# Attention with a soft mixture of experts on one core: small VectorE steps on one input stream, half of the low parts on GpSimd, mask and second fold split by head

## The chip, the cores and the metric

The kernel runs on one core of a Trainium2 chip. The core has five engines that work side by side, each through its own list of instructions in order: TensorE (PE in the profile, its weight loads PEld), VectorE (DVE), ScalarE (ACT), GpSimd (POOL) and SyncE (SP), which here issues all DMA transfers. They meet through semaphores. The metric is the time of one execution on the device, in microseconds (us).

## The reference

Eight sequences, eight heads, 576 positions, head dimension 64; then a soft mixture of eight experts with four slots each.

```python
scores = scale * np.matmul(q, k.transpose(0, 1, 3, 2))
cum = np.cumsum(np.maximum(s, 0.0), axis=-1)
bias = -(cum[:, :, :, None] - cum[:, :, None, :])
scores = np.where(causal, -1000000000.0, scores + np.minimum(bias, 0.0))
scores = scores - np.max(scores, axis=-1, keepdims=True)
attn = np.exp(scores)
attn = attn / (np.sum(attn, axis=-1, keepdims=True) + 1e-09)
attn_out = np.matmul(attn, v)
...
logits = x @ phi                       # x: (4608, 512), the heads side by side
d = softmax of logits over the rows    # dispatch; 32 columns
slot_input = d.T @ x
h = np.maximum(slot_input[e] @ w1[e], 0.0);  slot_out[e] = h @ w2[e]
c = softmax of logits over the columns # combine
out = c @ slot_out
```

## The kernel before, in words

Two heads (a = 0, 1) are one pair; there are 32 pairs p, four to a sequence, so eight batches b of four pairs. The attention loop runs over the pairs in a software pipeline and is followed by an expert part at the end. The names below are the keys of the operations (`op((name, p, ...), engine, ...)`) in the code.

For each pair: `load` brings q and k, transposed. `cast` (ACT) rounds them to the fast matmul format into a tile `w`, and `low` (line 453, DVE) subtracts, for queries (0) and keys (1), the rounded part from the original, so that products keep their accuracy: 64 calls on 128x576. `mx` (line 479, PE) makes approximate scores, four groups; `red` (line 493, DVE) adds the bias row `ub` from a DMA or, on the diagonal blocks, the masked copy `mk` of it, and takes the running maximum of each row. `mk` (line 432, POOL) makes that copy for both heads with two selects. `fm` (line 509, DVE) joins the two kinds of maximum into 20 columns `mh`; `f1` (line 514, PE) transposes them into `mt`; `f2` (ACT) and `f3` (line 524, DVE) split them in two parts `hl`; `md` writes these by DMA as extra rows beside the queries. Then `s` (line 550, PE) makes the scores with the maximum subtracted, `ex` (line 561, ACT) the exponentials, `cut` (line 568, POOL) zeroes what lies above the diagonal, `a` and `ax` (lines 643, 632, PE) multiply by the values.

The sums of the rows come from `za` (line 589), which adds two column blocks of the exponentials, head 0 on DVE and head 1 on POOL, from `z` (line 594, POOL), which folds in the third block from column group ZT = 4 on, both heads in one instruction of 2x320, and from `sm` (line 690, PE), which adds up the rest with a column of ones: 26 calls for a pair, which the profile counts as 52 matmuls. Every four pairs `e1` inverts the sums, a DMA pair `rw`, `rd` spreads them, `nr` (line 720, DVE) multiplies, and `nat`, `lt`, `c0` to `t8` update the expert logits and slots: `t2` (line 909) keeps the running minimum `nmin`, `t4` (line 927) the running sums `tot`, both on DVE with one or two columns.

What stands where in an engine's list is not written as a loop. A table gives each operation a place (a number for each kind, pair in the batch and type of batch), each engine's operations are sorted by it, and the function `timeline` merges the five lists with assumed durations, waits and a shared port of DVE and POOL. So the order inside each engine is fixed by the table alone. Short `busy` matmuls fill the start.

Of the kernel before, what the change touches and what calls it, by code (L numbers as in the profile page):

```python
# [13 lines left out]
ALU = mybir.AluOpType  # L14
# [11 lines left out]
ZT = 4  # L26
ZA = ("DVE", "POOL")

PERIOD = 38813
# [4 lines left out]
def table(text):  # L34
# [24 lines left out]
    low.0.0=-145512,-24218,-8235,-6404,-2495 cast.0.1=-128151,-13019,-9675,-10190,-5528
    low.0.1=-157331,-25864,-2554,-8208,-993 cum.0=-172132,3336,-5029,-2032,-7884  # L60
    mx.0.0=-131561,-13342,-2588,-8179,-2006 red.0.0.0=-130092,-17572,-1404,-3987,-2097
    red.0.0.1=-111753,-17989,-692,-3140,-2388 mx.0.1=-109409,-25895,-8267,-2275,-6484
    red.0.1.0=-120494,-22879,-3533,-2310,-5047 red.0.1.1=-132160,-23102,-3734,-2556,-7413
    mx.0.2=-182983,-12289,-790,795,1721 red.0.2.0=-115681,-15771,295,-165,1799 red.0.2.1=-113861,-5723,556,142,887
    mx.0.3=-90966,-2683,-739,1203,1628 red.0.3.0=-109993,-12133,974,107,756 red.0.3.1=-109885,-5704,1376,-210,1594
    fm.0=-109528,-2668,1624,1624,2297 f1.0=-86204,2876,7567,7523,10430 f2.0=-57637,-692,5807,5457,6581
    f3.0=-103916,3609,4834,2606,2954 md.0=-34002,9267,586,-1466,14239 s.0.0=-38951,14281,18571,20321,19184
    ex.0.0.0=-29427,16804,19505,18458,25033 ex.0.0.1=-26773,18031,19178,19412,23352
    cut.0.0=-105027,14062,17131,17024,21912 s.0.1=-44622,9375,15456,14386,18741
    ex.0.1.0=-39699,7602,18222,16186,22367 ex.0.1.1=-30923,10391,18102,17550,21966  # L70
    cut.0.1=-84485,8456,25066,19381,26094 s.0.2=-33057,17079,24080,22649,23834 ex.0.2.0=-9848,22550,24591,24608,28689
    ex.0.2.1=-9963,23174,24483,25538,28796 cut.0.2=-38055,14513,23950,20367,28508
    s.0.3=-38462,14628,23746,22649,21888 ex.0.3.0=-21484,18404,23936,21693,25606
    ex.0.3.1=-13247,21282,23727,23784,27494 cut.0.3=-38856,14194,18296,24860,31558
    za.0.0=-26432,23637,23749,21924,23432 za.0.1=-34684,18632,27777,25649,31493 z.0=-31754,20580,28351,30229,33192
    load_v.0=-166175,11282,12370,-153,12086 ax.0=-11237,23556,28279,25181,29500 evx.0=11009,23180,27183,29947,36125
    a.0.0=-30003,24119,25021,23376,25440 a.0.1=-15869,24133,26086,24741,28916 a.0.2=-15122,25617,27262,24978,30055
    a.0.3=-11096,26323,28058,25025,30813 a.0.4=-10535,26386,28379,25207,30960 ev.0=11844,28093,28120,30073,36400
    sm.0=678,27230,29412,29297,31087 rd.0=59666,61270,62920,64506,72341 nr.0=69670,70046,70115,69026,71358
    nat.0=69017,75129,73492,84383,78259 natd.0=69001,73241,77003,84760,98898  # L80
    load.1=-176331,-20047,-14277,-13193,-13109 ub.1=-79298,-9932,-9560,-9037,-8449
    mk.1=-112557,-14420,-2370,-6296,7120 cast.1.0=-125098,-4710,926,2478,3681 low.1.0=-135642,1399,7732,5391,2379
    cast.1.1=-90784,-2076,2080,3831,3729 low.1.1=-87008,5993,5799,5880,7841 cum.1=-75193,9964,6847,1104,17061
    mx.1.0=-65390,3350,10844,10876,12104 red.1.0.0=-66999,5531,7279,4194,7744 red.1.0.1=-59177,4739,7602,5128,6486
    mx.1.1=-48226,4979,11728,11495,13566 red.1.1.0=-81203,6332,7808,6343,9753 red.1.1.1=-72360,6946,8106,6446,10104
    mx.1.2=-44807,10990,15837,15272,14227 red.1.2.0=-58350,8322,12156,9208,11490
    red.1.2.1=-57220,8930,12813,12298,12329 mx.1.3=-73555,5275,15307,14146,15570
    red.1.3.0=-65406,7836,8773,6969,13629 red.1.3.1=-71098,9100,10270,8038,13444 fm.1=-56381,9503,13793,14035,15003
    f1.1=-40585,13083,18441,19461,19252 f2.1=-37646,16557,18858,18318,20199 f3.1=-48895,10151,14925,15709,15675
    md.1=-26222,12372,13204,11670,22553 s.1.0=-25920,23739,25038,23480,26146 ex.1.0.0=-1511,23454,24650,28195,32856  # L90
    ex.1.0.1=-766,25287,25010,28750,32245 cut.1.0=-33334,20326,28607,29130,41622 s.1.1=-26778,24442,25237,23677,26113
# [138 lines left out]
def tile_attn_softmoe(ctx: ExitStack, tc, qk, v, s, phi, w1, w2, cst, out):  # L230
# [10 lines left out]
    NCH = 5  # L241
# [133 lines left out]
    def own(kind, i, n):  # L375
        live[kind, i % n] = i
# [926 lines left out]
```

## Time and profile before

| | us |
|---|---|
| three runs: median, lowest, highest | 445.18, 443.41, 445.39 |
| the profiled execution, its own time | 443.02 |
| its span from first to last instruction | 441.2 |
| busy in it: PE / DVE / ACT / POOL | 398.7 / 355.4 / 240.3 / 218.2 |

The span is 1.8 us shorter than the execution's own time. The attention loop fills roughly the stretch from 35 to 346 us; from 381 us on the expert part runs. TensorE's granted clock was 0.978 over the whole span and 1.00 in the loop, its upper level, 2.4 GHz.

### The profile page before, as it was taken

Reading aid. Unit: us, or ns where it says so; the run is one execution under the profiler, and the core shown is the slowest. Engines: PE = TensorE matmul, PEld = TensorE weight load, DVE = VectorE, ACT = ScalarE, POOL = GpSimd, SP = SyncE. Lnnn points to the kernel's source line nnn. Section 1 sums busy time; section 2 is a strip of 40 time slices with the busy share of each in tenths; the row PEclk is TensorE's granted clock in tenths of the full one; section 3 lists DMA queues with packets and bytes.
Section 4 is the critical chain, followed back from the end, with each engine's and each line's share of the span. In section 5 each row is a group of like instructions: output and inputs, shape, how many; then the busy total and the mean of one; then the engine's idle time right before and its main releaser. Section 6 shows DMA issues by size and latency. Waiting matters only on the chain.

```text
span 441.2 us, 17319 instructions
## 1 busy us (share of the span) xinstructions
PE 398.7 (90%) x6667; PEld 282.7 (64%) x6667; DVE 355.4 (81%) x1515; ACT 240.3 (54%) x703; POOL 218.2 (49%) x320
## 2 busy tenths in 40 slices
PE   8899989988899989988999889899989997899950
PEld 7776666775577657856776567666756855435740
DVE  6899899889999999899999999889999285211460
ACT  4165656564676576855685549465764646011350
POOL 5558667446576665656664566476656610000000
PEclk9899999999999999999999999999999999899995
DMA  5645556666676667666775675474748979999898
GB/s 165 237 177 172 160 185 190 188 223 206 165 229 219 223 166 239 241 220 219 222 218 172 203 250 192 151 237 148 239 155 239 329 267 363 343 404 409 307 340 296
DMA packets 40290, 102.64 MB, mean 233 GB/s; under 512 B 5456, under 2 KB 15568, under 8 KB 40208
## 3 DMA queue, kind: packets, MB, share of 16 engines
q1 hardware_dynamic: 40208, 101.53, 68.7%
q8 instruction: 53, 0.87, 0.8%
q14 instruction: 29, 0.24, 0.2%
HBM read 90.98 MB, written 10.17 MB: 229 GB/s over the span
## 4 chain that ended last, share of the span: by engine, by line
PE 54%; DVE 25%; issue 8%; DMA 4%; ACT 3%; POOL 2%; DVEq 0%; SPq 0%; POOLq 0%; ACTq 0%
PE s L550 17%; DVE junk L493 11%; PE y L643 9%; PE mx L479 5%; PE sum L690 4%; PE m L1137 4%; DVE w L453 3%; PE m L1169 3%; DVE mh L509 3%; PE nat L728 3%; PE busy L1096 2%; DMA arena<-in_v_dram 2%; DMA arena<-rs 2%; DVE arena L589 1%; DVE arena L720 1%
## 5 line engine op out<-in xcount | busy, mean ns | idle before, releaser
L493 DVE CUSTOM_DVE_ANT_0 junk<-mx,arena 128x320 uint8<-128x320 f32 (+4 forms) x576 | 160.2, 335 | 16.8 <-PE mx L479 13.6
L561 ACT ACTIVATE arena<-s 128x288 f32<-128x288 f32 (+4 forms) x384 | 121.4, 394 | 53.1 <-PE s L550 48.8
L568 POOL TENSOR_SCALAR_AFFINE_SELECT arena<-arena 128x256 f32<-128x256 f32 (+1 forms) x160 | 68.4, 446 | 96.8 <-ACT arena L561 96.3
L550 PE MATMUL s<-w 64*128 64x288 f32 (+4 forms) x1152 | 111.9, 304 | 2.1 <-DVE e_nat L841 1.3
L643 PE MATMUL y<-arena 128*32 128x320 f32 (+4 forms) x1280 | 108.8, 427 | 0.6 <-POOL arena L568 0.5
L550 PEld LDWEIGHTS s<-w 64*128 64x128 f32 (+1 forms) x1152 | 84.1, 176 | 19.4 <-issue 8.3
L594 POOL TENSOR_TENSOR arena<-arena 128x640 f32<-128x640 f32 x31 | 51.8, 1671 | 22.8 <-DVE arena L589 19.8
L550 PE MATMUL s<-g 64*128 64x288 f32 (+4 forms) x384 | 60.1, 290 | 0.0
L453 DVE TENSOR_TENSOR w<-arena,w 128x576 fp32r<-128x576 f32 x64 | 57.8, 909 | 0.1
L432 POOL TENSOR_SCALAR_AFFINE_SELECT arena<-arena 128x640 f32<-128x640 f32 x64 | 49.9, 803 | 15.2 <-DMA arena<-cumu 11.5
L479 PE MATMUL mx<-w 64*128 64x448 f32 (+4 forms) x384 | 51.7, 317 | 0.7 <-ACT arena L561 0.3
L643 PEld LDWEIGHTS y<-arena 128*32 128x32 f32 x1280 | 37.1, 109 | 21.7 <-issue 14.0
L493 DVE DVE_READ_ACCUMULATOR2_ANT mx<- 128x1 f32 x576 | 45.9, 80 | 0.0
L448 ACT CAST w<-arena 128x576 fp32r<-128x576 f32 x64 | 41.6, 683 | 4.3 <-DMA arena<-in_qk_dram 3.8
L479 PEld LDWEIGHTS mx<-w 64*128 64x128 f32 x384 | 34.7, 184 | 14.3 <-ACT arena L561 3.0
L589 POOL TENSOR_TENSOR arena<-arena 128x448 f32<-128x448 f32 x31 | 38.1, 1230 | 3.2 <-PE sum L690 3.0
L550 PEld LDWEIGHTS s<-g 64*128 64x128 f32 (+1 forms) x384 | 38.4, 177 | 0.3
L690 PEld LDWEIGHTS sum<-arena,onesl 128*32 128x32 f32 x1664 | 28.3, 110 | 7.4 <-issue 5.0
L589 DVE TENSOR_TENSOR arena<-arena 128x448 f32<-128x448 f32 x33 | 30.8, 933 | 0.6 <-POOL arena L568 0.3
L690 PE MATMUL sum<-arena,onesl 128*32 128x64 f32 x1664 | 31.2, 220 | 0.0
L520 ACT CAST hi<-mt 20x128 fp32r<-20x128 f32 x32 | 8.1, 255 | 40.4 <-PE mt L514 40.1
L720 DVE TENSOR_TENSOR arena<-arena 128x576 f32<-128x576 f32 x31 | 27.3, 885 | 3.4 <-DMA arena<-rs 3.3
(160 smaller groups left out, 490.5 us busy)
## 6 DMA issues: line engine op xcount, KB each, us to landing
arena<-in_qk_dram SPq DMA_DIRECT2D x32, 576.0 KB
arena<-cumu SPq DMA_DIRECT2D x31, 576.0 KB
pre<-in_w_dram SPq DMA_DIRECT2D x29, 512.0 KB
arena<-in_w_dram SPq DMA_DIRECT2D x29, 512.0 KB
arena<-in_v_dram SPq DMA_DIRECT2D x32, 320.0 KB
arena<-rs SPq DMA_DIRECT2D x62, 144.0 KB
out_dram<-arena SPq DMA_DIRECT2D x12, 512.0 KB
out_dram<-pre SPq DMA_DIRECT2D x5, 512.0 KB
```

What stands on the lines that cost most here:

```text
L432: nc.gpsimd.affine_select(t[:, a], u[:, S * a:S * a + US], pattern=[[0, NCH], [-1, 128]], compare_op=ALU.is_ge, fill=NEG, base=0, channel_ ...
L448: nc.scalar.copy(w[:, QO + S * i:QO + S * (i + 1)], st["raw", p][:, i, :])
L453: nc.vector.tensor_tensor(w[:, QO + S * (2 + i):QO + S * (3 + i)], st["raw", p][:, i, :], w[:, QO + S * i:QO + S * (i + 1)].bitcast(F32), ...
L479: nc.tensor.matmul(ps[a][:, d:d + hi - lo], w[r, q0 - 128:q0], w[r, KO + lo:KO + hi], start=True, stop=True)
L493: nc.vector.tensor_tensor_reduce(out=junk[:, k + x:k + y], in0=ps[:, d + x - lo:d + y - lo], in1=bias(kind, a, x, y), scale=1.0, scalar=NE ...
L550: nc.tensor.matmul(ps[a][0:n, d:d + hi - lo], t[r, ko + 128 * j:ko + 128 * j + n], t[r, qo + lo:qo + hi], start=x == 0, stop=x == 3)
L561: nc.scalar.activation(st["p", p][0:n, a, o + lo:o + hi], ps[0:n, d:d + hi - lo], AF.Exp, bias=0.0, scale=0.125)
L568: nc.gpsimd.affine_select(d, d, pattern=[[0, 2], [1, n]], compare_op=ALU.is_ge, fill=0.0, base=0, channel_multiplier=-1)
L589: (nc.vector if ZA[a] == "DVE" or p == NP - 1 else nc.gpsimd).tensor_tensor(z[:, a], pt[:, a, 128:576], pt[:, a, 576:1024], op=ALU.add)
L594: (nc.vector if p == NP - 1 else nc.gpsimd).tensor_tensor(z, z, st["p", p][:, :, 1024 + SQ * ZT - 256:1344], op=ALU.add)
L643: nc.tensor.matmul(y[r, lo - 64:512], vt[:, j, r], st["p", p][:, i // 2, OFF[j] + lo - 128 * j:OFF[j] + 576 - 128 * j], start=(j == 0), st ...
L690: nc.tensor.matmul(y[o:o + 32, 0:SQ], onesl[:, 31 - row:63 - row], x(g), start=first and i == 0, stop=final and i == len(lists[f]) - 1)
```

## The change

- `low` of the keys (1) moves from DVE to POOL; that of the queries stays.
- `fm` becomes two `tensor_reduce` calls that read the 20 pairs of maxima as one input each, in place of one `tensor_tensor` with two inputs.
- `nmin` and `tot` become `tensor_scalar` with the second operand as a column of scalars; `tot` is two calls of one column in place of one of two.
- `mk` and `z` become one operation for each head; a `red` waits for the mask of its own head alone.
- ZT goes from 4 to 6: `z` covers 2 times 192 columns in place of 2x320, and `sm` takes 30 calls (60 matmuls in the profile's count) for a pair in place of 26.
- Some assumed durations of `timeline` and the whole table of places are new, so every engine's list is in a new order. The names stay; lines move by one to four.

```diff
-ZT = 4
+ZT = 6
+LOW = ("DVE", "POOL")
-PERIOD = 38813
+PERIOD = 39001
...
-    fm.0=-109528,-2668,1624,1624,2297 f1.0=-86204,2876,7567,7523,10430 f2.0=-57637,-692,5807,5457,6581
+    fm.0=-8878,4231,4143,4166,3921 f1.0=800,7372,5334,4640,4673 f2.0=797,2768,4696,3538,3886
...
-SHARED = ("low", "nr", "za", "z", "t2", "t4")
+SHARED = ("low", "nr", "za", "z")
...
-            for a in range(2):
-                nc.gpsimd.affine_select(t[:, a], u[:, S * a:S * a + US], pattern=[[0, NCH], [-1, 128]],
-                                        compare_op=ALU.is_ge, fill=NEG, base=0, channel_multiplier=1)
+            nc.gpsimd.affine_select(st["mk", p][:, a], u[:, S * a:S * a + US], pattern=[[0, NCH], [-1, 128]],
+                                    compare_op=ALU.is_ge, fill=NEG, base=0, channel_multiplier=1)
...
-            nc.vector.tensor_tensor(w[:, QO + S * (2 + i):QO + S * (3 + i)], st["raw", p][:, i, :],
+            (nc.vector if LOW[i] == "DVE" else nc.gpsimd).tensor_tensor(w[:, QO + S * (2 + i):QO + S * (3 + i)], st["raw", p][:, i, :],
...
-                   [("mx", p, i), ("ub", p), ("mk", p), dep("fm", old(3))], frees=[(("mx", p, i), a)])
+                   [("mx", p, i), ("ub", p), ("mk", p, a), dep("fm", old(3))], frees=[(("mx", p, i), a)])
...
-            x, y = (m[:, i].unsqueeze(2).broadcast_to([128, 2, 2, NCH]) for i in range(2))
-            nc.vector.tensor_tensor(mhs[p % 2].rearrange("p (a l c) -> p a l c", a=2, l=2), x, y, op=ALU.max)
+            for l in range(2):
+                nc.vector.tensor_reduce(mhs[p % 2].rearrange("p (a l c) -> p a l c", a=2, l=2)[:, :, l, :],
+                                        m.rearrange("p k a c -> p a c k"), axis=AX.X, op=ALU.max)
...
-            z = st["z", p][:, :, SQ * ZT - 128:448]
-            (nc.vector if p == NP - 1 else nc.gpsimd).tensor_tensor(z, z, st["p", p][:, :, 1024 + SQ * ZT - 256:1344], op=ALU.add)
+            z = st["z", p][:, a, SQ * ZT - 128:448]
+            (nc.vector if p == NP - 1 else nc.gpsimd).tensor_tensor(z, z, st["p", p][:, a, 1024 + SQ * ZT - 256:1344], op=ALU.add)
...
-            nc.vector.scalar_tensor_tensor(nmin[:, b % 2:b % 2 + 1], mm_[:, 0:1], -1.0, nmin[:, 1 - b % 2:2 - b % 2],
-                                           op0=ALU.mult, op1=ALU.min)
+            nc.vector.tensor_scalar(nmin[:, b % 2:b % 2 + 1], mm_[:, 0:1], -1.0, nmin[:, 1 - b % 2:2 - b % 2],
+                                    op0=ALU.mult, op1=ALU.min)
...
-            nc.vector.scalar_tensor_tensor(tot, tot, st["al", b], st.pop(("mm3", b))[:, 1:3], op0=ALU.mult, op1=ALU.add)
+            mm_ = st.pop(("mm3", b))
+            for i in range(2):
+                nc.vector.tensor_scalar(tot[:, i:i + 1], tot[:, i:i + 1], st["al", b], mm_[:, 1 + i:2 + i], op0=ALU.mult, op1=ALU.add)
```

Three places show how the lists move. The first is VectorE around `fm` of pair 18, in the fifth batch; `mh` is what `fm` writes, `hl` what `f3` writes, the 128x448 on the arena is `za`, the 128x576 on `w` is `low`, and the rows named ISA are `red` and its read-out. Before:

```order
L589 TENSOR_TENSOR arena<-arena 128x448
L453 TENSOR_TENSOR w_126<-arena,w_126 128x576
L509 TENSOR_TENSOR mh_112<-mx_102 128x20
L493 ISA junk,mx_104<-mx_19_0_3969,arena 128x128
L493 ISA mx_104 128x1
L493 ISA junk,mx_104<-mx_19_0_3969,arena 128x192
...
L927 SCALAR_TENSOR_TENSOR tot<-tot,al_3550,mm_3516 128x2
L524 SCALAR_TENSOR_TENSOR hl_4008<-hi_4006,nsel,mt 20x128
```

and now:

```order
L493 ISA junk,mx_102<-mx_18_1_3972,arena 128x128
L493 ISA mx_102 128x1
L509 TENSOR_REDUCE mh_112<-mx_102 128x2x5 x2
L931 TENSOR_SCALAR tot<-tot,al_3686,mm_3629 128x1 x2
L853 TENSOR_REDUCE cs_4040<-e_nat 128x5
L854 TENSOR_SCALAR cs_4040<-cs_4040 128x5
L855 RECIPROCAL cs_4040<-cs_4040 128x5
L590 TENSOR_TENSOR arena<-arena 128x448
L453 TENSOR_TENSOR w_126<-arena,w_126 128x576
L525 SCALAR_TENSOR_TENSOR hl_4098<-hi_4089,nsel,mt 20x128
```

`fm` now stands directly behind the last `red` of its pair, `za` and the one `low` have moved behind it, and `f3` stands behind those two.

The second is TensorE at the same pair; `mt` is the transpose `f1` that waits for `fm`, `y` is `a`. Before:

```order
L479 MATMUL mx_19_1_3970<-w_126 128x320
L643 MATMUL y_3912<-arena 32x448 x4
L514 MATMUL mt<-ident,mh_112 20x128
L550 MATMUL s_2_0_3996<-w_128 128x448
L550 MATMUL s_2_1_3997<-w_128 128x448
```

and now:

```order
L551 MATMUL s_0_0_4046<-g_123 128x192
L551 MATMUL s_0_1_4047<-g_123 128x192
L515 MATMUL mt<-ident,mh_112 20x128
L645 MATMUL y_4074<-arena 32x512 x4
L634 MATMUL x_4084<-arena 32x64 x4
```

The transpose now stands between score products and the products with the values, where it stood between products with the values and score products.

The third is GpSimd around pairs 16 to 18; 64x2x64 and 128x2x128 are `cut`, 128x640 `mk`, 128x448 `za` of head 1. Before:

```order
L568 AFFINE_SELECT arena<-arena 64x2x64
L594 TENSOR_TENSOR arena<-arena 128x2x320
L568 AFFINE_SELECT arena<-arena 128x2x128 x2
L432 AFFINE_SELECT arena<-arena 128x640 x2
L568 AFFINE_SELECT arena<-arena 128x2x128 x2
L568 AFFINE_SELECT arena<-arena 64x2x64
L589 TENSOR_TENSOR arena<-arena 128x448
L594 TENSOR_TENSOR arena<-arena 128x2x320
```

and now:

```order
L453 TENSOR_TENSOR w_128<-arena,w_128 128x576
L595 TENSOR_TENSOR arena<-arena 128x192 x2
L453 TENSOR_TENSOR w_124<-arena,w_124 128x576
L431 AFFINE_SELECT arena<-arena 128x640 x2
L569 AFFINE_SELECT arena<-arena 64x2x64
L569 AFFINE_SELECT arena<-arena 128x2x128 x4
L595 TENSOR_TENSOR arena<-arena 128x192
L590 TENSOR_TENSOR arena<-arena 128x448
L595 TENSOR_TENSOR arena<-arena 128x192
```

The keys' `low` of pairs 17 and 18 (the 128x576 on `w`) now stands in this list, on either side of the two short folds of pair 15, and the folds of a pair stand apart, each behind or ahead of `za` by its head.

## Rows read from the trace of the kernel before

**Rows 1.** The page: busy us (share of span) xinstructions; the last chain.

```profile
PE 398.7 (90%) x6667; PEld 282.7 (64%) x6667; DVE 355.4 (81%) x1515; ACT 240.3 (54%) x703; POOL 218.2 (49%) x320
PE 54%; DVE 25%; issue 8%; DMA 4%; ACT 3%; POOL 2%; DVEq 0%; SPq 0%; POOLq 0%; ACTq 0%
```

**Rows 2.** The loop: us, busy of PE, PEld, DVE, ACT, POOL, clock, DMA, GB/s.

```profile
35.00:346.00 311.00, 292.90 (x5383) 210.27 (x5379) 291.57 (x1281) 194.94 (x582) 191.24 (x268) 1.00 0.64 204
```

**Rows 3.** Waits of TensorE: us in total, times, longest us.

```profile
PE mt L514 <- DVE mh L509: 14.1, 13, 1.5
PE s L550 <- DVE e_nat L841: 1.3, 1, 1.3
PE y L643 <- POOL arena L568: 0.5, 1, 0.5
PEld mt L514 <- DVE mh L509: 2.2, 2, 1.7
PEld y L643 <- issue: 14.0, 64, 0.3
```

**Rows 4.** Order of time at pair 18: start us, us, engine, line.

```profile
200.24 1.92 POOL L594 TENSOR_TENSOR arena<-arena 128x640 f32<-128x640 f32 x1 [0.63 <-PE mx L479]
200.68 1.51 DVE L509 TENSOR_TENSOR mh<-mx 128x20 f32<-128x20 f32 x1
202.34 0.27 PE L514 MATMUL mt<-ident,mh 128*20 128x128 f32 x1 [1.27 <-DVE mh L509]
```

**Rows 5.** The same near 92 us.

```profile
91.51 1.55 POOL L594 TENSOR_TENSOR arena<-arena 128x640 f32<-128x640 f32 x1 [0.72 <-DVE arena L589]
91.66 1.42 DVE L909 SCALAR_TENSOR_TENSOR nmin<-mm,nmin 128x1 f32<-128x1 f32 x1
93.82 0.33 PE L550 MATMUL s<-w 64*64 64x64 f32 x5 [1.30 <-DVE e_nat L841]
```

**Rows 6.** Groups by line on DVE: xcount, busy us, mean ns, idle before.

```profile
L453 DVE TENSOR_TENSOR w<-arena,w 128x576 fp32r<-128x576 f32 x64 | 57.8, 909 | 0.1
L589 DVE TENSOR_TENSOR arena<-arena 128x448 f32<-128x448 f32 x33 | 30.8, 933 | 0.6 <-POOL arena L568 0.3
L720 DVE TENSOR_TENSOR arena<-arena 128x576 f32<-128x576 f32 x31 | 27.3, 885 | 3.4 <-DMA arena<-rs 3.3
L509 DVE TENSOR_TENSOR mh<-mx 128x20 f32<-128x20 f32 x32 | 18.1, 567 | 0.6
L909 DVE SCALAR_TENSOR_TENSOR nmin<-mm,nmin 128x1 f32<-128x1 f32 x8 | 7.6, 945 | 0.3
L927 DVE SCALAR_TENSOR_TENSOR tot<-tot,al,mm 128x2 f32<-128x2 f32 x8 | 4.1, 508 | 0.0
L331 DVE TENSOR_REDUCE nsel<-ident 20x1 f32<-20x10 f32 x1 | 0.1, 126 | 0.0
```

**Rows 7.** Single lines on DVE: duration ns min/median/max, first and last start.

```profile
L509 DVE TENSOR_TENSOR mh<-mx x32: 139/245/1510, 17.0 to 340.9; 128x20 f32<-128x20 f32 x32
L453 DVE TENSOR_TENSOR w<-arena,w x64: 695/753/2227, 7.2 to 330.5; 128x576 fp32r<-128x576 f32 x64
L909 DVE SCALAR_TENSOR_TENSOR nmin<-mm,nmin x8: 159/1415/1418, 91.7 to 370.4; 128x1 f32<-128x1 f32 x8
L852 DVE TENSOR_SCALAR cs<-cs x8: 171/172/385, 134.6 to 373.6; 128x5 f32<-128x5 f32 x8
L524 DVE SCALAR_TENSOR_TENSOR hl<-hi,nsel,mt x32: 326/329/337, 17.8 to 342.2; 20x128 fp32r<-20x128 f32 x32
```

**Rows 8.** Groups by line on POOL and `sm` on PE.

```profile
L594 POOL TENSOR_TENSOR arena<-arena 128x640 f32<-128x640 f32 x31 | 51.8, 1671 | 22.8 <-DVE arena L589 19.8 <-PE mx L479 2.5
L589 POOL TENSOR_TENSOR arena<-arena 128x448 f32<-128x448 f32 x31 | 38.1, 1230 | 3.2 <-PE sum L690 3.0
L690 PE MATMUL sum<-arena,onesl 128*32 128x64 f32 x1664 | 31.2, 220 | 0.0
```

**Rows 9.** VectorE at the start, its first `red`.

```profile
12.08 0.29 DVE L493 CUSTOM_DVE_ANT_0 junk<-mx,arena 128x128 uint8<-128x128 f32 x1 [2.78 <-POOL arena L432]
```

More of the change, by code (lines that the diff above doesn't have):

```diff
@@ L59 @@
[L59 to L64, printed above, removed]
@@ L82 @@
[L82 to L86, printed above, removed]
@@ L87 @@
[L87 to L91, printed above, removed]
@@ new lines @@
+    cast.0.0=-38335,-7162,-7932,-6265,-6674 low.0.0=-27886,1602,2894,4175,3981
+    cast.0.1=-28601,-8592,-5485,-10603,-4663 low.0.1=-17238,2816,-2429,-2486,288 cum.0=10020,-3787,-1478,-1309,7736
+    mx.0.0=-20603,273,-2850,-3122,-3508 red.0.0.0=-20161,-2585,139,-1953,-2729 red.0.0.1=-21564,-1516,144,-1760,-2850
+    mx.0.1=-7681,909,-1896,-2309,-2634 red.0.1.0=-15314,-1466,270,-25,-1380 red.0.1.1=-26871,1404,569,-1064,-1530
+    mx.0.2=-16204,2381,732,1768,1537 red.0.2.0=-15464,2528,3856,3607,3471 red.0.2.1=-22950,2601,3263,1800,1978
@@ new lines @@
+    ub.1=1970,-2973,-1818,-884,1300 mk.1.0=-7538,7513,6083,2267,3500 mk.1.1=16145,8553,5361,4834,1535
+    cast.1.0=-16985,2237,1310,2494,2921 low.1.0=-14366,7706,4494,4194,4722 cast.1.1=-3005,2752,1664,1124,2926
+    low.1.1=25287,17909,18101,10945,8662 cum.1=1822,8928,1199,8346,7021 mx.1.0=-3408,9957,8102,8001,8811
+    red.1.0.0=860,9129,9780,8727,10157 red.1.0.1=5432,8831,9831,9092,9351 mx.1.1=-1011,7737,6790,6473,7585
+    red.1.1.0=-290,8011,7576,8377,8068 red.1.1.1=5574,8764,9012,8540,8734 mx.1.2=2879,11115,11190,11251,10246
@@ new lines @@
+    natd.1=74673,75332,75223,78472,59592 load.2=6104,8598,1265,5384,3865 ub.2=13242,9159,1534,7057,2834
+    mk.2.0=26313,14796,12960,13056,9224 mk.2.1=26498,14414,13096,14177,11271 cast.2.0=4775,12990,13048,13991,14321
+    low.2.0=10192,22588,22873,26174,25966 cast.2.1=3163,13297,15037,14351,15034 low.2.1=26672,18816,22842,21202,17530
+    cum.2=23916,13470,11039,8344,10200 mx.2.0=8053,15048,13868,14794,14092 red.2.0.0=7755,14533,15890,14994,18949
+    red.2.0.1=8677,13068,16600,16196,20119 mx.2.1=12474,15254,15770,16609,14666
@@ L441, in scores @@
         g = old(NM)
-        war = [("red", g, i, a) for i in range(4) for a in range(2)] if g is not None else []
-        op(("mk", p), "POOL", 1330, mk, [("ub", p)] + war)
+        for a in range(2):
+            war = [("red", g, i, a) for i in range(4)] if g is not None else []
+            op(("mk", p, a), "POOL", 690, (mk, a), [("ub", p)] + war)
         def cast(i):
@@ L458, in scores @@
             op(("cast", p, i), "ACT", 565, (cast, i), [("load", p)] + war)
-            op(("low", p, i), "DVE", 670, (low, i), [("cast", p, i)])
+            op(("low", p, i), LOW[i], 620 if LOW[i] == "DVE" else 1370, (low, i), [("cast", p, i)])
         def cum_in():
@@ L573, in scores @@
         g = old(NBUF["p"])
-        war = [("a", g, j) for j in range(5)] + [("ax", g), ("za", g, 0), ("za", g, 1), ("z", g) if ZT < 9 else None, ("sm", g)] if g is not None else []
+        war = [("a", g, j) for j in range(5)] + [("ax", g), ("za", g, 0), ("za", g, 1), *((("z", g, 0), ("z", g, 1)) if ZT < 9 else ()), ("sm", g)] if g is not None else []
         for i in range(4):
@@ L580, in scores @@
                    frees=[(("s", p, i), a)])
-            op(("cut", p, i), "POOL", cutt[i], (cut, i), [("ex", p, i, 0), ("ex", p, i, 1)])
+            op(("cut", p, i), "POOL", cutt[i] + 10, (cut, i), [("ex", p, i, 0), ("ex", p, i, 1)])
         def za(a):
             use("p", p, NBUF["p"])
-            if a == 0:
+            if ("z", p) not in st:
                 own("z", p, NBUF["z"])
@@ L597, in scores @@
             e = "DVE" if p == NP - 1 else ZA[a]
-            op(("za", p, a), e, 490 if e == "DVE" else 1060, (za, a),
-               [("ex", p, i, a) for i in range(2)] + [("cut", p, 2), ("sm", g) if g is not None else None, ("za", p, 0) if a else None])
+            op(("za", p, a), e, 534 if e == "DVE" else 1080, (za, a),
+               [("ex", p, i, a) for i in range(2)] + [("cut", p, 2), ("sm", g) if g is not None else None, ("za", p, 0) if a and ZA[0] == ZA[1] else None])
         if ZT < 9:
             n = 9 - ZT
-            op(("z", p), "DVE" if p == NP - 1 else "POOL", 50 + 134 * n if p == NP - 1 else 306 * n, zs,
-               [("cut", p, 3), ("za", p, 0), ("za", p, 1)])
+            for a in range(2):
+                op(("z", p, a), "DVE" if p == NP - 1 else "POOL", 45 + 67 * n if p == NP - 1 else 20 + 155 * n, (zs, a),
+                   [("cut", p, 3), ("za", p, a)])
     def groups_of(b):
@@ L753, in pair @@
         op(("sm", p), "PE", {4: 760, 6: 865, 9: 1080}[ZT], sm,
-           [("z", p) if ZT < 9 else None, ("za", p, 1), ("cut", p, 3), ("cut", p, 0), ("cut", p, 1), ("pads",), prev, ("sm", p - 1) if p else None], ldw=27, tail=27, mode=3)
+           [*((("z", p, 0), ("z", p, 1)) if ZT < 9 else ()), ("za", p, 0), ("za", p, 1), ("cut", p, 3), ("cut", p, 0), ("cut", p, 1), ("pads",), prev, ("sm", p - 1) if p else None], ldw=27, tail=27, mode=3)
         if not direct:
```

208 lines of the change are left out of this document (104 added, 104 removed).

## The prediction

> **What bounds the kernel now.** I read the page first: TensorE is busy for 398.7 us of the 441.2 us span, VectorE for 355.4, GpSimd only for 218.2, and the chain that ended last runs 54% over TensorE and 25% over VectorE [rows 1]. So two engines share the bound, and it has to be read in the loop alone. From 35 to 346 us TensorE is busy for 292.9 of 311 us and VectorE for 291.6, 94% each, GpSimd for 191.2 (61%), and DMA has a share of 0.64 [rows 2]. TensorE's clock is 1.00 there, so no change of clock is to be had. Next the list of waits: TensorE waited for `fm` ("mh") 13 times for 14.1 us, its weight loads twice more for 2.2 us; it waited once for 1.3 us for a VectorE step that frees a bank, and hardly for GpSimd's `cut` (0.5 us) [rows 3]. TensorE's recorded idle time in the loop is 311 - 292.9 = 18.1 us, and these waits, 16.3 + 1.3 us, are about as much. That is the main reading: `fm`, a step on 20 columns, causes nearly all idle time that TensorE shows.
>
> Why it is slow is seen in the order of time. At pair 18 the fold `z` ran on GpSimd from 200.24 to 202.16 us; `fm` started on VectorE at 200.68 and took 1.51 us, until `z` was over, and the transpose had waited 1.27 us for it at 202.34 [rows 4]. The same near 92 us: `z` from 91.51 for 1.55 us, `nmin`, one column, from 91.66 for 1.42 us, and behind it TensorE idle for 1.30 us [rows 5]. Unhindered, `fm` takes 139 ns and `nmin` 159 ns, and their longest are 1510 and 1418 [rows 7]. Both read two inputs from SBUF. `f3`, which has one tensor input in SBUF and one in PSUM, took 326 to 337 ns in all 32 calls [rows 7]: it never waited. So a VectorE step with two SBUF inputs stands still while a GpSimd step is under way, and one with a single such input does not.
>
> **The change part by part.** The sum is made against the profiled execution's own 443.0 us, which is 2.2 us below the median of the three runs.
>
> `fm` as two reductions. The nearest row is a reduction over 20x10 elements, 126 ns [rows 6]; two of them are about 0.25 us, where `fm` now takes 0.567 us on the mean of 32 [rows 6]. VectorE saves 32 x 0.31 = 10 us. For TensorE the 15 stalls, 16.3 us, are what counts [rows 3]: bounds are all of it, or nothing if what stands ahead of `fm` on VectorE is as late. The new list answers that: `za` and `low`, both of two inputs, stood ahead of `fm` at pair 18 and now stand behind it. I leave 15 x 0.25 = 3.8 us and take **-12.5**. What becomes late next is `f3`, which at this place moves behind `za` and the one `low`; its DMA `md` starts some 1.5 us later behind `fm` than it could, and `s` of that pair waits for it.
>
> `nmin` and `tot`. `nmin` takes 0.945 us on the mean and could take 0.159, `tot` 0.508 [rows 6, 7]; a `tensor_scalar` on five columns takes 172 ns as a rule and 385 at most [rows 7]. So VectorE saves 8 x 0.77 = 6 us and 8 x (0.508 - 2 x 0.172) = 1.3 us. TensorE felt it in one recorded wait of 1.3 us [rows 3, 5]; bounds 0 and 7.5, taken **-1.5**.
>
> The Trainium skill, page "SBUF — State Buffer", section "Who interferes with whom", says that a VectorE instruction with two SBUF inputs and a GpSimd instruction that reads SBUF exclude each other for the whole of the one that came first; the trace agrees (1.51 us of wait for 139 ns of work). The same section says that a `tensor_scalar` can itself run in a mode that takes the shared port, which speaks against this part. The trace agrees at most in part: 385 against 172 ns, a wait of 0.2 us, not of 1.26. By the rule alone the -1.5 would be 0.
>
> `low` of the keys. VectorE loses 32 calls of 0.909 us, 29 us with their waits, or 32 x 0.695 = 22 us without [rows 6, 7]. GpSimd's additions cost 1.230 us for 448 and 1.671 for 640 columns [rows 8], 2.30 ns a column, so 576 columns are 1.52 us and 32 of them +49 us. The split `z` is 2 x (1.230 - 256 x 0.0023) = 1.28 us in place of 1.67, 31 x -0.39 = -12 us. GpSimd gains 37 us of work and had 311 - 191 = 120 us free in the loop [rows 2], which is the cover; without it every us on that list would delay `s` or `cut`. VectorE's own list shortens by 10 + 6 + 1 + 29 = 46 us, from 94% to about 79% of the loop. What that is worth on TensorE is not seen in its idle time; the busy time has modelled ends and can hide waits for banks that a late `red` frees. Bounds 0 and -8; taken **-2**.
>
> `sm`. 1664 matmuls take 31.2 us [rows 8]; they go in rounds over four groups of 32 rows, seven rounds for a pair now and eight with ZT = 6, so 31.2 / 7 = **+4.5** on TensorE, which nothing covers.
>
> The order. Counted in the two lists up to the expert part, TensorE changes between kinds of matmul (transposes, score products, products with the values and sums) 196 times in place of 227. A change shows as idle time of the weight loads: 14.0 us over 64 times, 0.22 us each [rows 3]. 31 x 0.22 = 6.8 us is the most, 0 the least; taken **-3**, since the matmuls still in flight cover a part.
>
> The masks by head. At the start the first `red` waited 2.78 us for `mk` [rows 9]; its head's half is ready half of `mk` earlier: **-0.7**. In the loop these waits are not among the large ones.
>
> GpSimd's fuller list. `cut` stands behind `low` now and then; TensorE's waits for it were 0.5 us [rows 3]. Bounds 0 and 14 (all that the rest gains); taken **+1.5**.
>
> Sum: -12.5 - 1.5 - 2 + 4.5 - 3 - 0.7 + 1.5 = -13.7; 443.0 - 13.7 = 429.3. As the profiled run lies below the median, I forecast **430 us**. The transfers of weights behind the loop start when the loop's buffers come free, so they shift with it, and the share of 0.64 [rows 2] leaves room for the earlier ones.
>
> **The rivals.** *VectorE was the bound.* For it: 94% busy, a quarter of the chain [rows 1, 2]. Against it: TensorE is as busy. Then the 46 us come back until TensorE is full: all 18.1 us of idle and the 6.8 us of changes, with +4.5 and -0.7, 443.0 - 21 = 422, with waits hidden in TensorE's busy time 418.
>
> *Keys' low parts come late (not faster).* `low` of pair 17 stands on GpSimd ahead of the folds of pair 15, in order with everything else, and all four `s` of a pair wait for it. Now the low parts wait for nothing on VectorE but the port. If `s` is held up 0.43 us a pair, 32 x 0.43 = 13.7 us, nothing is left: 443. Against it: by the lists each stands about a pair ahead of its use.
>
> *The port is the bound (slower).* Work that excludes each other: GpSimd 191.2 us [rows 2] and the two-input steps of VectorE unhindered, 64 x 0.753 [rows 7], 31 x 0.753 of `nr` and 33 x 0.59 of `za` (by columns), 32 x 0.139: 95 us, together 286 of 311 us. Afterwards 191 + 37 + 95 - 24 - 4 = 295. At today's ratio the loop becomes 311 x 295 / 286 = 321: +10, so 453. It decides if the waits of VectorE's two-input steps, now (57.8 - 48.2 + 30.8 - 19.3 + 27.3 - 23.3) / 128 = 0.19 us each [rows 6], grow by 46 / 96 = 0.48 us and eat all that VectorE saves. For it: the hold of a `low` doubles, 0.753 to 1.52 us, in the same hands as `cut`. Against it: the short steps no longer pay it, and both engines had idle or waiting time in which these holds overlap. The skill's rule above is what makes this a rival.
>
> *The reductions wait after all.* Then only the order and `low` pay: 430 + 12.5 = 442. Against it: `f3` never waited [rows 7].
>
> **How the numbers follow.** Forecast, 424 to 437: 0.57. VectorE as the bound, 418 to 423: 0.13. Late low parts, 438 to 446: 0.14. The port, 446 to 455: 0.09. Reductions that wait, 439 to 444: 0.07. Range 418 to 442, with some 0.05 below and 0.15 above. A measurement here can tell about 0.5%, 2.2 us, from no change. Faster by more, below 443.0: 0.57 + 0.13 and some two thirds of the late parts and the waiting reductions, 0.83; within: 0.08; slower: 0.09.
>
> **What would show it.** Right: line 509 at about 130 ns a call with no long ones, `nmin` under 0.4 us, TensorE's wait for "mh" under 5 us; VectorE's share of the loop down by some 15 points, GpSimd's up by 10, TensorE's up; `sm` on 1920 matmuls. Wrong: TensorE's waits move to `low` on GpSimd, to `hl` or to `cut`; or `za`, `nr` and the queries' `low` on VectorE take over 1.1 us on the mean. A loop that is shorter while the end behind it is longer would say that DMA held the weights back.

## The result and the profile after

The changed kernel took 430.09 us (median of three runs, 428.18 to 431.42) against 445.18: a ratio of 0.967, 95% interval 0.960 to 0.974. A second set on the same chip as two of the experiments gave 428.62 us (425.67 to 430.35, six runs) and 0.964 (0.959 to 0.969). The execution profiled below is the slowest of the first three, 431.42 us with a span of 429.7, 11.5 us less than before. The whole of that is gone before the expert part: its first long group of matmuls starts at 369.2 us in place of 380.8, and what follows takes as long as before.

The page and the loop, in the columns of [rows 1, 2]:

```profile
PE 398.9 (93%) x6911; PEld 288.1 (67%) x6911; DVE 313.1 (73%) x1524; ACT 238.4 (55%) x703; POOL 247.2 (58%) x383
```

```profile
35.00:346.00 311.00, 304.18 (x5866) 223.87 (x5862) 256.94 (x1306) 201.64 (x611) 221.01 (x333) 1.00 0.68 216
```

In the same 311 us TensorE is busy for 304.2 in place of 292.9 us, 98%, VectorE for 256.9 in place of 291.6 and GpSimd for 221.0 in place of 191.2. The loop now ends earlier, so the last 14 us of this stretch hold less of it. In the part of the stretch that holds the loop in both, from 35 to 332 us, VectorE goes from 279.2 to 251.5 us, 94% to 85%, and GpSimd from 182.6 to 216.4, 61% to 73%.

The waits of TensorE and of its weight loads, which answer to [rows 3]:

```profile
PE mt L515 <- DVE mh L509: 3.6, 7, 1.3
PE x L634 <- DVE mx L493: 1.8, 1, 1.8
```

```profile
PEld y L645 <- issue: 13.2, 55, 0.5
PEld mt L515 <- DVE mh L509: 2.0, 3, 0.9
```

The waits for `fm` fell from 14.1 + 2.2 to 3.6 + 2.0 us. The 14.0 us that the loads lost at the start of products with the values became 13.2.

Pair 18 in order of time, as in [rows 4], with more of VectorE (columns: start us, us, engine, line):

```profile
188.15 1.45 POOL L431 TENSOR_SCALAR_AFFINE_SELECT arena<-arena 128x640 f32<-128x640 f32 x2
...
190.09 0.75 DVE L453 TENSOR_TENSOR w<-arena,w 128x576 fp32r<-128x576 f32 x1
...
191.61 0.25 DVE L509 TENSOR_REDUCE mh<-mx 128x10 f32<-128x20 f32 x2
...
194.12 0.80 DVE L590 TENSOR_TENSOR arena<-arena 128x448 f32<-128x448 f32 x1 [1.24 <-POOL arena L569]
194.21 0.28 PE L515 MATMUL mt<-ident,mh 128*20 128x128 f32 x1
...
194.85 0.74 DVE L453 TENSOR_TENSOR w<-arena,w 128x576 fp32r<-128x576 f32 x1
...
195.76 0.33 DVE L525 SCALAR_TENSOR_TENSOR hl<-hi,nsel,mt 20x128 fp32r<-20x128 f32 x1 [0.17 <-ACT hi L521]
```

`fm` ran at 191.61 us in 0.25 us, and its transpose at 194.21 waited for nothing. `za` and the one `low` now stand between `fm` and `f3` (line 525), which ends 4.2 us behind `fm`. For `f3` TensorE and its weight loads waited 0.2 + 0.5 us in all, less than the 0.5 + 1.4 us before.

Groups by line, as in [rows 6, 8], VectorE first:

```profile
L722 DVE TENSOR_TENSOR arena<-arena 128x576 f32<-128x576 f32 x31 | 31.7, 1038 | 5.8 <-DMA arena<-rs 5.8
L453 DVE TENSOR_TENSOR w<-arena,w 128x576 fp32r<-128x576 f32 x32 | 28.8, 904 | 3.8 <-ACT w L448 3.8
L590 DVE TENSOR_TENSOR arena<-arena 128x448 f32<-128x448 f32 x33 | 24.1, 732 | 8.0 <-POOL arena L569 7.4 <-PE sum L692 0.2
L509 DVE TENSOR_REDUCE mh<-mx 128x10 f32<-128x20 f32 x64 | 8.1, 168 | 0.8
L931 DVE TENSOR_SCALAR tot<-tot,al,mm 128x1 f32<-128x1 f32 x16 | 3.6, 265 | 0.0
L911 DVE TENSOR_SCALAR nmin<-mm,nmin 128x1 f32<-128x1 f32 x8 | 1.7, 214 | 0.3
```

```profile
L453 POOL TENSOR_TENSOR w<-arena,w 128x576 fp32r<-128x576 f32 x32 | 45.4, 1419 | 0.2
L595 POOL TENSOR_TENSOR arena<-arena 128x192 f32<-128x192 f32 x62 | 41.5, 680 | 26.5 <-DVE arena L590 25.7
```

```profile
L692 PE MATMUL sum<-arena,onesl 128*32 128x64 f32 x1920 | 34.6, 220 | 0.0
```

And single calls, min/median/max, as in [rows 7]:

```profile
L509 DVE TENSOR_REDUCE mh<-mx x64: 133/166/176, 17.5 to 326.6; 128x10 f32<-128x20 f32 x64
L911 DVE TENSOR_SCALAR nmin<-mm,nmin x8: 213/214/214, 90.6 to 357.9; 128x1 f32<-128x1 f32 x8
L854 DVE TENSOR_SCALAR cs<-cs x8: 171/198/1462, 98.0 to 361.6; 128x5 f32<-128x5 f32 x8
```

No call of line 509 took more than 176 ns, none of `nmin` more than 214. VectorE's other steps of two inputs still wait: `low` at 904 ns a call as before, `za` less (732 against 933), `nr` (line 722) more (1038 against 885). Worked out as for the port in the prediction, their wait is (28.8 - 24.1 + 24.1 - 19.3 + 31.7 - 23.3) / 96 = 0.19 us each, as before.

### The profile page after: what moved, and what is told of

Its sections match the earlier page's. It is cut to its first block, busy times and chain, and to the rows that moved or that the text cites. A ratio compares the mean times of both kernels' runs of the same rounds, so it can differ in the third digit from the quotient of the medians.

```text
span 429.7 us, 17835 instructions
## 1 busy us (share of the span) xinstructions
PE 398.9 (93%) x6911; PEld 288.1 (67%) x6911; DVE 313.1 (73%) x1524; ACT 238.4 (55%) x703; POOL 247.2 (58%) x383
## 5 line engine op out<-in xcount | busy, mean ns | idle before, releaser
L493 DVE CUSTOM_DVE_ANT_0 junk<-mx,arena 128x128 uint8<-128x128 f32 (+4 forms) x576 | 159.1, 335 | 25.2 <-PE mx L479 24.5
L645 PE MATMUL y<-arena 128*32 128x320 f32 (+4 forms) x1280 | 101.8, 426 | 0.3 <-issue 0.3
L569 POOL TENSOR_SCALAR_AFFINE_SELECT arena<-arena 128x256 f32<-128x256 f32 (+1 forms) x160 | 61.8, 405 | 62.6 <-ACT arena L562 62.3
L551 PEld LDWEIGHTS s<-w 64*128 64x128 f32 (+1 forms) x1152 | 87.3, 179 | 7.7 <-issue 1.7
L595 POOL TENSOR_TENSOR arena<-arena 128x192 f32<-128x192 f32 x62 | 41.5, 680 | 26.5 <-DVE arena L590 25.7
L645 PEld LDWEIGHTS y<-arena 128*32 128x32 f32 x1280 | 36.1, 109 | 24.5 <-issue 13.2
L453 POOL TENSOR_TENSOR w<-arena,w 128x576 fp32r<-128x576 f32 x32 | 45.4, 1419 | 0.2
L722 DVE TENSOR_TENSOR arena<-arena 128x576 f32<-128x576 f32 x31 | 31.7, 1038 | 5.8 <-DMA arena<-rs 5.8
L692 PE MATMUL sum<-arena,onesl 128*32 128x64 f32 x1920 | 34.6, 220 | 0.0
L453 DVE TENSOR_TENSOR w<-arena,w 128x576 fp32r<-128x576 f32 x32 | 28.8, 904 | 3.8 <-ACT w L448 3.8
L590 DVE TENSOR_TENSOR arena<-arena 128x448 f32<-128x448 f32 x33 | 24.1, 732 | 8.0 <-POOL arena L569 7.4
```

The costliest lines, as they stand in the source:

```text
L453: (nc.vector if LOW[i] == "DVE" else nc.gpsimd).tensor_tensor(w[:, QO + S * (2 + i):QO + S * (3 + i)], st["raw", p][:, i, :], w[:, QO + S ...
L493: nc.vector.tensor_tensor_reduce(out=junk[:, k + x:k + y], in0=ps[:, d + x - lo:d + y - lo], in1=bias(kind, a, x, y), scale=1.0, scalar=NE ...
L551: nc.tensor.matmul(ps[a][0:n, d:d + hi - lo], t[r, ko + 128 * j:ko + 128 * j + n], t[r, qo + lo:qo + hi], start=x == 0, stop=x == 3)
L569: nc.gpsimd.affine_select(d, d, pattern=[[0, 2], [1, n]], compare_op=ALU.is_ge, fill=0.0, base=0, channel_multiplier=-1)
L590: (nc.vector if ZA[a] == "DVE" or p == NP - 1 else nc.gpsimd).tensor_tensor(z[:, a], pt[:, a, 128:576], pt[:, a, 576:1024], op=ALU.add)
L595: (nc.vector if p == NP - 1 else nc.gpsimd).tensor_tensor(z, z, st["p", p][:, a, 1024 + SQ * ZT - 256:1344], op=ALU.add)
```

## The experiments

Each ran six times or more beside the kernel before on the same chip; ratios are to it. Two theories stood against the prediction's (A: the waits behind `fm`): B, that VectorE's whole load was the bound, and C, that the new order is the gain.

**fm alone.** The kernel before with the one edit:

```diff
-            nc.vector.tensor_tensor(mhs[p % 2].rearrange("p (a l c) -> p a l c", a=2, l=2), x, y, op=ALU.max)
+            for l in range(2):
+                nc.vector.tensor_reduce(mhs[p % 2].rearrange("p (a l c) -> p a l c", a=2, l=2)[:, :, l, :],
+                                        m.rearrange("p k a c -> p a c k"), axis=AX.X, op=ALU.max)
```

> The kernel before with one edit: fm as two reductions; everything else, the order too, as before. Theory A (TensorE's waits for fm behind GpSimd's folds cost the 12 to 14 us): line 509 at 130 to 170 ns with no long call, TensorE's wait for mh from 14.1 to under 5 us, the time 8 to 13 us below the kernel before (ratio 0.971 to 0.982). Rival B (VectorE's whole load was the bound, and low of the keys is most of the gain): fm alone saves VectorE 10 of 46 us, so 2 to 4 us (ratio 0.991 to 0.996). Rival C (the new order is the gain): 0 to 3 us.

438.16 us, ratio 0.983 (0.980 to 0.987): -7.5 us. Pair 18 in its order of time, and TensorE's waits:

```profile
196.91 0.74 DVE L453 TENSOR_TENSOR w<-arena,w 128x576 fp32r<-128x576 f32 x1
197.13 1.94 POOL L595 TENSOR_TENSOR arena<-arena 128x640 f32<-128x640 f32 x1 [0.63 <-PE mx L479]
197.58 0.24 DVE L509 TENSOR_REDUCE mh<-mx 128x10 f32<-128x20 f32 x2
```

```profile
PE mt L515 <- DVE mh L509: 7.5, 8, 1.6
```

The reductions ran in 0.24 us in the middle of a `z` of 1.94 us: in the same place as in [rows 4], with 1.51 us there. But TensorE still waits 7.5 us for `fm`, 8 times, more than the "under 5" of theory A: the step itself no longer waits, but what stands ahead of it is late. In four of the eight, 4.4 us, it stands directly behind a `low` of 0.79 to 2.23 us; two, 2.4 us, lie at the start, at 17 and 25 us, behind `red`, and the other two, 0.8 us, stand behind `red` too. The time gained lies just below theory A's 8 to 13 us and far from B and C.

The trace of the kernel before shows the same division. In five of its 13 waits for `fm`, 5.6 of the 14.1 us, `fm` itself took no more than 0.18 us, as here at 190.63 us behind a `low` of 2.23:

```profile
188.48 2.23 DVE L453 TENSOR_TENSOR w<-arena,w 128x576 fp32r<-128x576 f32 x1
190.63 0.17 DVE L509 TENSOR_TENSOR mh<-mx 128x20 f32<-128x20 f32 x1
190.94 0.27 PE L514 MATMUL mt<-ident,mh 128*20 128x128 f32 x1 [1.17 <-DVE mh L509]
```

In the other eight `fm` took 0.42 to 1.51 us. What it took above 0.18 us, up to the length of each wait, is 7.3 us, near the 7.5 us that the edit gained.

**fm put back in the changed kernel.** The same diff the other way, in the new order.

> The changed kernel with fm put back to one step with two inputs, in the new order. Theory A: the long calls of line 509 come back, TensorE waits for mh again, 8 to 13 us above the changed kernel (438 to 443 us). Rival B: 1 to 3 us above it. Rival C: the order puts fm where GpSimd is not in the way, so no more than 2 us above it.

438.40 us, ratio 0.983 (0.979 to 0.988), 0.016 to 0.020 above the changed kernel by its two sets (0.967 and 0.964), 7 to 9 us. Line 509 there, and TensorE's waits for it, 3.6 us in the changed kernel:

```profile
L509 DVE TENSOR_TENSOR mh<-mx x32: 167/185/3651, 17.0 to 334.4; 128x20 f32<-128x20 f32 x32
```

```profile
PE mt L514 <- DVE mh L509: 8.8, 10, 3.0
```

So the new order alone does not keep `fm` out of GpSimd's way. The call of 3.65 us, from 144.85 us on, stood beside a `low`, two halves of `z` and another `low` on GpSimd. Both directions give about 8 us for `fm`.

**All three small steps.** The kernel before with `fm`, and with

```diff
-            nc.vector.scalar_tensor_tensor(nmin[:, b % 2:b % 2 + 1], mm_[:, 0:1], -1.0, nmin[:, 1 - b % 2:2 - b % 2],
-                                           op0=ALU.mult, op1=ALU.min)
+            nc.vector.tensor_scalar(nmin[:, b % 2:b % 2 + 1], mm_[:, 0:1], -1.0, nmin[:, 1 - b % 2:2 - b % 2],
+                                    op0=ALU.mult, op1=ALU.min)
...
-            nc.vector.scalar_tensor_tensor(tot, tot, st["al", b], st.pop(("mm3", b))[:, 1:3], op0=ALU.mult, op1=ALU.add)
+            mm_ = st.pop(("mm3", b))
+            for i in range(2):
+                nc.vector.tensor_scalar(tot[:, i:i + 1], tot[:, i:i + 1], st["al", b], mm_[:, 1 + i:2 + i], op0=ALU.mult, op1=ALU.add)
```

> The kernel before with the three small edits alone: fm as reductions, nmin and tot as tensor_scalar; order, low, masks and folds as before. With fm alone at 0.983 of the kernel before: if nmin's waits reach TensorE as forecast (1.5 us), 0.980; if most of the five long calls of nmin reach it, 6 us, 0.970; if they don't, 0.983. nmin and tot themselves at 170 to 270 ns with no long call.

433.95 us, ratio 0.976 (0.971 to 0.981), 0.007 below `fm` alone, 3.2 us. The half-widths of the two, 0.004 and 0.005, add in squares to 0.006, so this is only just told apart, and `nmin` and `tot` were not tried one by one. With `fm` alone `nmin` still stood like this, 6 us of waiting on VectorE in all:

```profile
L910 DVE SCALAR_TENSOR_TENSOR nmin<-mm,nmin 128x1 f32<-128x1 f32 x8 | 7.8, 975 | 0.3
```

**Low of the keys back on VectorE**, in the changed kernel, directly behind the queries' one:

```diff
-LOW = ("DVE", "POOL")
+LOW = ("DVE", "DVE")
-    low.3.1= ...
+    low.3.1= (the row of low.3.0; so for the four pairs)
```

> The changed kernel with both low steps of a pair on VectorE, the keys' one directly behind the queries' in the list. Theory A: VectorE's share of the loop rises by about 8 points and GpSimd's falls by 13, TensorE hardly feels it: 429 to 434 us. Rival B: VectorE is full again and 6 to 10 us come back, 436 to 440 us. Rival D (the port held longer by low on GpSimd costs something): 2 us or more below the changed kernel.

440.24 us, ratio 0.989 (0.985 to 0.992), 0.022 to 0.025 above the changed kernel: 10 to 11 us come back. Its loop, and who waits for `f3`:

```profile
35.00:346.00 311.00, 300.27 (x5690) 216.28 (x5687) 274.07 (x1322) 195.00 (x587) 187.03 (x297) 1.00 0.65 209
```

```profile
PE s L551 <- DVE hl L525: 3.7, 6, 0.9
PEld s L551 <- DVE hl L525: 5.7, 7, 1.1
```

VectorE is at 88%, not full; TensorE's idle time is 10.7 us in place of 6.8. Its waits for `hl` went from 0.7 us in the changed kernel (0.2 on TensorE, 0.5 on its loads) to 9.4: `f3` now stands behind `za` and two `low`. So in this order, with the keys' `low` in this place on VectorE, the step on GpSimd is worth 10 us, as rival B had it. These waits point to the place of one step, `f3`, and not to a full engine; no run moved `f3` or that `low` alone, so this is read from the waits and not shown.

**All edits in the old order.** The changed code with the old table; the halves of `mk` and `z` have the place of the one instruction.

```diff
-    mk.0.0=-19966,... mk.0.1=-20993,...     (the new table)
+    mk.0.0=-114088,... mk.0.1=-114088,...   (the old one, mk.0 and z.0 twice)
```

> All edits of the change in the order of before: the old table of places, the two halves of mk and z side by side where the one instruction stood, low of the keys on GpSimd sorted in by its old place. Theory A: most of the gain without the order, 430 to 435 us. Rival C: the order is the gain, 440 us or more. Between, 435 to 440, the two share it.

471.75 us, ratio 1.059 (1.054 to 1.064): 26 us slower than before. First SyncE's waits, then waits of VectorE and TensorE:

```profile
SPq L395 <- POOL w L455: 31.6, 9, 5.2
SPq L395 <- POOL arena L571: 22.8, 9, 9.8
```

```profile
DVE junk L495 <- PE mx L481: 42.8, 39, 5.8
PE mt L517 <- DVE mh L511: 16.1, 9, 3.7
```

The load of a later pair (line 395) waits for both `low` of the pair whose buffer it takes. On GpSimd, in a place that was chosen for VectorE, `low` is late; the load waits 31.6 us for it in all (and 22.8 us more by the profile for `cut`, a step of the same list), the transfers behind it on SyncE wait too, then the scores and `red`. From 35 to 346 us TensorE was busy for 284.0 us at a granted clock of 0.95, in place of 292.9 us at 1.00 in the kernel before; how much of the 26 us is the clock, no run separates. In the changed kernel the load's wait for `low` is a fifth:

```profile
SPq L393 <- POOL w L453: 6.7, 3, 5.3
SPq L393 <- POOL arena L569: 2.2, 5, 0.8
```

**All edits but low, in the old order:** the same table with `LOW = ("DVE", "DVE")`.

> All edits but low, in the order of before: what cost 41 us in the run of all edits in the old order is told apart. If it was the keys' low on GpSimd in a place that was chosen for VectorE: 434 to 440 us, near the run with fm alone (438.2), plus 3 for sm, less 1 to 2 for nmin and tot. If the split folds and masks or sm do not fit the old order: 445 us or more.

434.11 us, ratio 0.976 (0.970 to 0.982). Taking `low` back gains 38 us: `low` on GpSimd was the cost of the run above, and nothing else in it. The load's wait for `low`, on VectorE again, is half:

```profile
SPq L395 <- DVE w L455: 14.9, 14, 2.6
```

This kernel is as fast as the three small steps alone (0.976).

**The same with ZT = 4.** One line, `ZT = 6` to `ZT = 4`.

> All edits but low and but ZT, in the order of before (ZT = 4 as before, masks and folds by head). Against the run with ZT = 6 in the same order (0.976): if sm's cost on TensorE decides, 3 to 4.5 us less, 0.967; if the shorter fold is worth as much, the same. Against the run with the three small edits alone: if the split by head is worth something in the old order, below it by 1 us or more.

435.50 us, ratio 0.978 (0.972 to 0.983). In the old order neither the longer `sm` with the shorter fold (0.976 against 0.978) nor the split by head (0.978 against 0.976 for the small steps) can be told from nothing.

**ZT = 4 in the changed kernel.** The same line there.

> The changed kernel with ZT back to 4: the folds are 2 x 320 columns in place of 2 x 192, and sm takes 52 matmuls a pair in place of 60. If sm's cost is as I took it and GpSimd's 12 us more are covered: 4 to 5 us below the changed kernel, 425 to 426. If GpSimd's load is no longer covered (73% of the loop, low at 1.42 us in the same list): 430 to 436.

430.87 us, ratio 0.974 (0.970 to 0.977), 0.007 to 0.010 above the changed kernel, 3 to 4 us. Against the first of its two sets that lies within the interval, and so does the difference to the run without the step on `cs` below (0.969), on the same chip. The halves of `z` cost 944 ns each in place of 680, 16 us more on GpSimd:

```profile
L595 POOL TENSOR_TENSOR arena<-arena 128x320 f32<-128x320 f32 x62 | 57.8, 944 | 30.3 <-DVE arena L590 29.5
```

In this order the shorter fold is worth at least what `sm` costs; that it is worth more is likely but not firmly shown.

**None of the edits in the new order.** The kernel before with the new table; the keys' `low` behind the queries' one, `mk` at the earlier and `z` at the later place of its halves.

> None of the edits, but the new table of places: both low on VectorE, the keys' one directly behind the queries' one, one instruction for mk and z at the earlier place of the two halves for mk and the later for z. If the edits' effects add up in the new order (8.3 for fm by the run with fm back, 10 for low by the run with low on VectorE, less 3.5 for sm): 443 to 447 us, no gain from the order by itself. If the order by itself is worth something: 435 to 441.

440.42 us, ratio 0.993 (0.990 to 0.997). The order alone is worth 0.7%, 3 us, so C's share is small.

The effects do not add up. The run with both `low` on VectorE is this kernel with all other edits, `fm` and the longer `sm` among them, and lies at 0.989: 0.005 lower, 2 us, with a half-width of 0.005, hardly told from nothing. The waits of TensorE and its loads for `fm` fell there from 7.5 + 8.5 to 3.6 + 1.4 us, but those for `f3` stayed, 3.1 + 5.1 here and 3.7 + 5.7 there. In the same order with the keys' `low` on GpSimd `fm` is worth 7 to 9 us. So a wait that goes is a gain only where no other wait takes its place.

**Without the step on cs.** In the changed kernel:

```diff
-            nc.vector.tensor_scalar(cs, cs, 1e-9, None, op0=ALU.add)
```

This leaves out an addition that changes nothing in single precision, since the sums are at least 1.

> The changed kernel without the step that adds 1e-9 to the sums cs of the second softmax (line 854; the sums are at least 1, so it changes nothing in single precision). That step took 435 ns on the mean of 8 and 1462 once, beside a low on GpSimd. If such waits on VectorE no longer reach TensorE: within 1 us of the changed kernel. If they do: 1.5 to 3.5 us less.

429.50 us, ratio 0.969 (0.964 to 0.974): no difference to the changed kernel can be told.

**The changed kernel once more**, with no edit.

> The changed kernel itself, to have it on the same chip as the other two: 0.967 of the kernel before, as before, between 0.962 and 0.972. If the run with the small edits in the old order is within 0.004 of it, low on GpSimd and the new order together are worth nothing measurable; if it is 0.01 or more above, they are worth 4.5 us or more.

0.964, as said above. Against the run of all edits but `low` in the old order, 0.976 with a half-width of 0.006, it is 0.012 lower, 5 us (2 to 9 by the two intervals): this is what `low` on GpSimd and the new order give together. Neither gives it alone: `low` without the order loses 38 us, the order without `low` is slower than the old one by 0.013. No version tried beats the changed kernel.

## Why the prediction was right, and where its terms were not

The time lies on the forecast, 430.1 against 430, but several terms were wrong and cancelled: that it lies so close is luck.

- *What bounds it.* Right. TensorE's idle time in the loop went from 18.1 to 6.8 us and its busy time to 98%. The port as the bound and late low parts did not decide in the changed kernel (the waits of the two-input steps stayed at 0.19 us each); the run in the old order shows that the second is real, +38 us, and that the place in GpSimd's list is what holds it off.
- *`fm`, -12.5.* The mechanism is shown, by both runs; the size was too large, 7 to 9 us measured. The step that failed is counting all but 3.8 of the 16.3 us of waits as `fm`'s own, from the total and one place in the order of time. In the trace of before 5.6 us of them stand behind an `fm` of 0.18 us at most, and two of the 13, 2.2 us, lie at 17 and 25 us, ahead of the loop whose idle time they were set against. With `fm` alone changed, 7.5 us remained on TensorE. Part of that goes only with the new order, where 3.6 + 2.0 us are left; "under 5" holds for TensorE and is missed by 0.6 with its loads. With both `low` on VectorE in the new order all edits together gave only 2 us, `fm` among them, which the term, a fixed price, could not say.
- *`nmin` and `tot`, -1.5.* Mis-sized the other way: 3.2 us, just told apart. TensorE's one recorded wait of 1.3 us was not all that five stalls of 1.26 us cost. Behind each of the five stands `f3` within three steps; that its lateness is the rest is not shown.
- *`low` -2, order -3, GpSimd's list +1.5*, together -3.5. Together about 5 us were measured. They were wrong as separate terms: there is no cost of `low` without a place in the lists. The order's -3 was priced by idle time of the weight loads at changes between kinds of matmul; the row it was taken from went only from 14.0 to 13.2 us, with the order alone as in the changed kernel, so hardly any of what the order gives is that. `f3` was forecast to be late next: it does end 4.2 us behind `fm`, but TensorE and its loads waited only 0.7 us for it; with two `low` ahead of it, 9.4 us.
- *`sm`, +4.5.* Its price on TensorE is there, 31.2 to 34.6 us busy, +3.4. As a part of the sum it failed: with the shorter `z` the edit cost nothing that can be told in the old order, and nothing in the new, where it perhaps gained 3 to 4 us. GpSimd's 120 us of idle time in the loop were taken as cover for whatever its list does, and `z` stands right ahead of `sm`. A shorter `z` also shortens what VectorE's steps wait for: with ZT = 4 in the changed kernel `low` took 995 ns on the mean in place of 904 and `nr` 1182 in place of 1038.
- *Masks, -0.7.* Not seen: the first `red` started at 12.05 us against 12.08. It no longer waited for a mask but for the approximate scores `mx`, which TensorE in its new order ended at 11.89 us in place of 10.36:

```profile
12.05 0.29 DVE L493 CUSTOM_DVE_ANT_0 junk<-mx,arena 128x128 uint8<-128x128 f32 x1 [4.09 <-PE mx L479]
```

- *VectorE saves 46 us.* 42.3 us in the whole span, 355.4 to 313.1. Its share fell by 9 points to 332 us (11 in the prediction's own stretch to 346), not 15: in the same stretch there is now more of the loop's work, and `nr` waits more.
- *GpSimd's prices.* `low` 1.42 us against 1.52 worked out, a half of `z` 0.68 against 0.64.

What stays open is how the 5 us divide between `low` on GpSimd and the order, which only exist together, whether another place for the keys' `low` on VectorE would do as well in the new order, and whether the split by head gives anything in the new order; it was not tried by itself there.

## What to carry to other kernels

Look for short steps whose longest call is ten times their shortest; when a step of another engine spans the excess, a form that reads one tensor input may remove it, as the reductions did in all 64 calls (line 854 below, of one input, still waited). Before that, look at every wait that you count: in this case `fm` was short in five of the 13, so about half of the time was not its own. Work moved to an engine with idle time needs a place of its own there: the same `low` on GpSimd, against its place on VectorE, was worth -10 us in one order and +38 in another.

## What was not expected of the hardware

A waiting VectorE step lost to several GpSimd steps in a row, not to one alone. In the changed kernel `nr`, 755 ns as a rule, took 4.34 us from 116.26 us on and ended at 120.60, 0.6 us behind the last of a row of GpSimd steps, six of them at the least (the three `cut` and the two `mk` are merged rows):

```profile
115.50 1.01 POOL L569 TENSOR_SCALAR_AFFINE_SELECT arena<-arena 128x256 f32<-128x256 f32 x3 [0.45 <-ACT arena L562]
116.26 4.34 DVE L722 TENSOR_TENSOR arena<-arena 128x576 f32<-128x576 f32 x1
116.48 1.14 POOL L590 TENSOR_TENSOR arena<-arena 128x448 f32<-128x448 f32 x1
117.57 0.46 POOL L861 TENSOR_TENSOR e_nat<-e_nat,cs 128x160 f32<-128x160 f32 x1
117.98 0.60 POOL L595 TENSOR_TENSOR arena<-arena 128x192 f32<-128x192 f32 x1
118.53 1.46 POOL L431 TENSOR_SCALAR_AFFINE_SELECT arena<-arena 128x640 f32<-128x640 f32 x2
```

And a `tensor_scalar` waited as well: line 854, five columns by a constant, 171 ns at its shortest and 198 at the median, took 1.46 us beside a `low` on GpSimd:

```profile
98.00 1.46 DVE L854 TENSOR_SCALAR cs<-cs 128x5 f32<-128x5 f32 x1
98.02 1.41 POOL L453 TENSOR_TENSOR w<-arena,w 128x576 fp32r<-128x576 f32 x1
```

The forms of `nmin` and `tot`, one column with one or two columns of scalars, took 213 to 214 and 260 to 269 ns in all their calls. So the rule of the Trainium skill, page "SBUF — State Buffer", section "Who interferes with whom", that a `tensor_scalar` can take the shared port, agrees with this trace for the first form, more than the 0.2 us that the prediction read from the kernel before; for the second no call here shows it. Why these two forms differ, no run here shows.
